# Later rounding and subtraction of the gated tokens, a shared ring of four activation buffers, and operands in a pool of their own

## The chip, the core and the metric

The kernel runs on one core of a Trainium2 chip. The metric is the device time of one execution in microseconds (us). An execution is a little longer than the span of the trace, which runs from the core's first instruction to its last.

The core's engines work side by side, each through its own queue and in order: TensorE (PE in the profile; its weight loads are shown apart as PEld), VectorE (DVE), ScalarE (ACT), GpSimd (POOL) and SyncE (SP), which here issues most of the DMAs. An instruction at the head of a queue that waits for another engine holds up all that stands behind it on its own engine.

## What is computed

A long convolution by Fourier transforms, gated with x, and then two two-layer networks over 24,960 tokens of 128 features, with 2,048 hidden features each:

```python
y = irfft(rfft(x * v, n=2*S) * rfft(h_filt, n=2*S))[:, :S]   # (2, 12480, 128)
a = x * y                                                    # the gate
h = a @ w_in1                                                # 128 -> 2048
g = h * clip(h + 3, 0, 6) / 6
b = g @ w_out1                                               # 2048 -> 128
h = maximum(b @ w_in2, 0)
out = (h * h) @ w_out2
```

## The kernel before

**Up to about 465 us** the kernel computes the filter and the forward and middle transforms. What follows is one long loop, and the change lies in it.

**Tokens.** The last step of the convolution makes the tokens in 64 blocks j of 390. For a block, `combine` adds and subtracts two loaded halves (`pp`, `pn`; DVE for j below 3, POOL after), `s4` runs 8 small float32 matmuls into a PSUM bank `py` (the trace shows each as two, 16 in all), and `gate` (L530) multiplies `py` by x in place (DVE, L532) and rounds it to the tile's high part `oh` (ACT, L534). `gate_rest` (L536) subtracts that from `py` to get the low part `ol` (DVE, L540). The networks take tiles of 512 tokens (the first one 390, the last one 506), so a block may fall into two tiles, and some tiles need two new blocks.

**Steps.** A step n is one tile and one of 8 slices of 256 hidden features (`NP` = 8 steps a tile). In the loop at L721 a step stands in this order: `l1(n)` (6 matmuls into the bank `ph`: weights low by high part, high by low, high by high, for two halves), `l2(n - 3)` (6 matmuls into the tile's bank `acc`), `finish` of a tile, the jobs in `early_do`, `relu(n)` (ACT), `act(n)` (DVE), `split(n - 1)` (ACT rounds `gh`; DVE or POOL subtracts `gl`, L643), the jobs in `late_do`, and one piece of `late`, which decodes the second network's weights until about 860 us. The engines take these in that order, each its own.

**Tiles.** The first 14 tiles are of network 1 alone; after that tiles of network 1 and network 2 alternate, and at the end there are 14 of network 2.

**The jobs of a block** are set by a table (L558 to L584): `s4` begins at a step n0 + q of the tile before (n0 is that tile's first step), at one of three rates, and is done 1, 2 or 4 steps later, at step `done`. `gate` stands in `early_do` of `done`, `gate_rest` in `early_do` of the step after, or of `done` itself at rate 1. Rate 1 is used behind the first 14 tiles for the first block of a tile that needs two; there are ten such tiles, at n0 = 128, 192, 240, 288, 336, 384, 448, 496, 544 and 592. Among the first 14 tiles four with two blocks stand at n0 = 24, 48, 72 and 96; their first block is begun at n0 and done at n0 + 1.

**A shared bank.** `py` and `acc` share two PSUM banks (`bank`, L506). A tile's first `l2` (at step n0 + 3) can't begin before the block that last used its bank has been read for the last time, which `gate_rest` does.

**Buffers.** `relu` writes `r` (2 buffers), `act` writes `g` (2), `split` writes `gh` and `gl` (3 each). All of them, `oh`, `ol` and the loaded blocks lie in one pool, `moe`.

Of the kernel before, what the change touches and what calls it, by code (L numbers as in the profile page):

```python
# [7 lines left out]
F32 = mybir.dt.float32  # L8
F32R = mybir.dt.float32r
U32 = mybir.dt.uint32  # L10
AF = mybir.ActivationFunctionType
ALU = mybir.AluOpType
# [19 lines left out]
TM = 512  # L32
# [11 lines left out]
def tile_hyena_moe(ctx: ExitStack, tc, xg, vg, xT, pos, w1d, w2d, fmat, fwin, twc,  # L44
                   tws, twcf, twsf, dcs, inv, vtab, w_in1, w_out1, w_in2, w_out2, out):
    nc = tc.nc
# [234 lines left out]
    with tc.tile_pool(name="mlp", bufs=2, side="right") as mp, \  # L281
# [40 lines left out]
        for c in range(16):  # L322
# [10 lines left out]
            for q in range(4):  # L333
                ov = hs[q][:N1].rearrange("p d (h a) -> p a h d", h=2)
                src = fps[:N1, :, :, 32 * q:32 * q + 32]
# [32 lines left out]
    def idle(ps, count):  # L368
        for _ in range(count):
            nc.tensor.matmul(ps[:, 0, :TOK], wh[0][:, 0, :128], wh[0][:, 0, :TOK])  # L370
# [4 lines left out]
    with tc.tile_pool(name="cv_ps", bufs=4, space=PSUM) as vps:  # L375
# [17 lines left out]
        for i in range(NI + 2):  # L393
# [19 lines left out]
            elif late_rows:  # L413
                blk, h, sv = late_rows.pop(0)
# [4 lines left out]
            for t, f in ((a + 6, load), (a + 3, product)):  # L419
                g, s = divmod(t, 3)  # L420
# [21 lines left out]
    early.close()  # L442


    mo = ctx.enter_context(tc.tile_pool(name="moe", bufs=2))
    mps = ctx.enter_context(tc.tile_pool(name="moe_ps", bufs=2, space=PSUM))
    zt, pm, xin = {0: (za, zb)}, {}, {}

    def inputs(t):
        if (0, t) not in xin:  # L450
            xin[(0, t)] = tuple(mo.tile([128, TM], F32R, name=f"o{p}{t}", tag=f"o{p}", bufs=3)
                                for p in "hl")
        return xin[(0, t)]

    inputs(0)
    ends = [TOK]
    while ends[-1] < NTOK:
        ends.append(min(ends[-1] + TM, NTOK))
# [14 lines left out]
    LAG = 3  # L473
# [30 lines left out]
    py = {}  # L504
# [19 lines left out]
    def ranges(j):  # L524
        for t in range(NTI):
            lo, hi = max(TOK * j, begins[t]), min(TOK * j + TOK, ends[t])
            if lo < hi:
                yield t, slice(lo - TOK * j, hi - TOK * j), slice(lo - begins[t], hi - begins[t])

    def gate(j):  # L530
        ps = py[j]
        nc.vector.tensor_tensor(ps[:, :TOK], ps[:, :TOK], xt.pop(j), ALU.mult)  # L532
        for t, src, dst in ranges(j):
            nc.scalar.activation(inputs(t)[0][:, dst], ps[:, src], AF.Copy)  # L534

    def gate_rest(j):  # L536
        ps = py.pop(j)
        for t, src, dst in ranges(j):
            h, l = xin[(0, t)]
            nc.vector.tensor_tensor(l[:, dst], ps[:, src], h[:, dst].bitcast(F32),  # L540
                                    ALU.subtract)

    begun, early_do, late_do = {}, {}, {}

    def plan(table, n, f, *args):
        table.setdefault(n, []).append((f, args))
# [7 lines left out]
    for t in range(1, NTI):  # L554
        js = list(range(last[t - 1] + 1, last[t] + 1))
        i = place_of[(0, t - 1)]
        n0, fast = NP * i, place_of[(0, t)] == i + 1
        if t == 1:  # L558
            jobs = [(js[0], 2, 2, i + 1), (js[1], 4, 2, i + 1)]
        else:  # L560
            jobs = [(js[-1], 4, 2 if fast else 0, i + 1)]
            if len(js) > 1:
                jobs.insert(0, (js[0], 0, 2 if fast else 1, i))
        assert len(js) == len(jobs)
        for j, q, rate, k in jobs:
            n = n0 + q
            plan(begun, n, s4, j, k)
            begun[n][-1] += (rate,)
            done = n + (4, 2, 1)[rate]
            gated[j] = done  # L570
            plan(early_do, done, gate, j)
            plan(early_do, done + (rate != 1), gate_rest, j)
            if j < 3:
                lead = (2, 1)
            elif j < 4:
                lead = (6, 5)
            else:
                lead = (7, 5)
            for back in lead:
                plan(late_do, n - back, combining, j)  # L580
            if j == 3:
                plan(late_do, 0, loads, j)
            elif j > 3:
                plan(late_do, gated[j - 3] + 1, loads, j)  # L584
# [12 lines left out]
    ph, rs, gs, gh, acc = ({} for _ in range(5))  # L597
# [15 lines left out]

    def relu(n):
        w = size[steps[n][1]]
        r = mo.tile([128, 2, TM], F32, name=f"r{n}", tag="r", bufs=2)
        if steps[n][0] == 0:
            nc.scalar.activation(r[:, :, :w], ph[n][:, :, :w], AF.Relu, bias=three)  # L618
        else:
            nc.scalar.activation(r[:, :, :w], ph[n][:, :, :w], AF.Relu)  # L620
        rs[n] = r

    def act(n):
        w = size[steps[n][1]]
        r, pv = rs.pop(n)[:, :, :w], ph.pop(n)[:, :, :w]
        gt = mo.tile([128, 2, TM], F32, name=f"g{n}", tag="g", bufs=2)
        g = gt[:, :, :w]
        if steps[n][0] == 0:
            nc.vector.scalar_tensor_tensor(g, r, 6.0, pv, ALU.min, ALU.mult)  # L629
        else:  # L630

            nc.vector.scalar_tensor_tensor(g, pv, 0.0, r, ALU.max, ALU.mult)  # L632
        gs[n] = g

    def split(n):
        g, w = gs.pop(n), size[steps[n][1]]
        h = mo.tile([128, 2, TM], F32R, name=f"gh{n}", tag="gh", bufs=LAG)[:, :, :w]
        l = mo.tile([128, 2, TM], F32R, name=f"gl{n}", tag="gl", bufs=LAG)[:, :, :w]
        nc.scalar.activation(h, g, AF.Copy)  # L639
        on_vector = (0, 3, 6) if n < NP * AHEAD else (0, 2, 4, 6)  # L640

        eng = nc.vector if n < NP or steps[n][2] in on_vector else nc.gpsimd
        eng.tensor_tensor(l, g, h.bitcast(F32), ALU.subtract)  # L643
        gh[n] = (h, l)
# [55 lines left out]
    decode(2, 1)  # L700
    decode(0, 3)
    gate(0)
    gate_rest(0)
    idle(mps.tile([128, 2, 512], F32, name="idle1", tag="ph", bufs=3), 6)
    decode(1, 3)
    decode(2, 6)
# [14 lines left out]
    for n in range(len(steps) + LAG + 1):  # L721
        if n < len(steps):
            l, j, q = steps[n]
            l1(n)
        m = n - LAG
        if 0 <= m < len(steps):
            l2(m)
        if 0 <= m - 1 < len(steps) and steps[m - 1][2] == NP - 1:
            finish(*steps[m - 1][:2])
        for f, args in early_do.pop(n, ()):  # L730
            f(*args)
        if n < len(steps):
            if q == 6 and n + 2 < len(steps) and steps[n + 2][0] == 1:
                part1(steps[n + 2][1])
            relu(n)
            act(n)
        if 0 <= n - 1 < len(steps):
            split(n - 1)
        for f, args in late_do.pop(n, ()):
            f(*args)  # L740
        for _ in range(2 if n < 14 else 1):
            next(rest, None)
# [94 lines left out]
```

## Time and profile before

| what | us |
|---|---|
| median of 3 runs | 2806.07 (2804.76 to 2806.34) |
| the profiled execution, its own time | 2803.87 |
| its span | 2801.7 |
| PE busy | 2742.1 (98%) |
| DVE busy | 1994.6 (71%) |
| ACT busy | 1931.6 (69%) |
| POOL busy | 1508.3 (54%) |

In a row of the trace the columns are the start, the duration, the engine, the line, the operation, what it writes and reads, and how many; in brackets stands the idle time of the engine before it, with who ended it. A matmul of 512 columns is shown with 0.39 us although the next one starts about 0.23 us later: they are pipelined, and the ends are modelled. Busy shares are means over stages with different limits, so windows and single waits say more than the totals.

### The profile page before, as it was taken

Reading aid. Unit: us, or ns where it says so; the run is one execution under the profiler, and the core shown is the slowest. Engines: PE = TensorE matmul, PEld = TensorE weight load, DVE = VectorE, ACT = ScalarE, POOL = GpSimd, SP = SyncE. Lnnn points to the kernel's source line nnn. Section 1 sums busy time; section 2 is a strip of 40 time slices with the busy share of each in tenths; the row PEclk is TensorE's granted clock in tenths of the full one; section 3 lists DMA queues with packets and bytes.
Section 4 is the critical chain, followed back from the end, with each engine's and each line's share of the span. In section 5 each row is a group of like instructions: output and inputs, shape, how many; then the busy total and the mean of one; then the engine's idle time right before and its main releaser. Section 6 shows DMA issues by size and latency. Waiting matters only on the chain.

```text
span 2801.7 us, 34821 instructions
## 1 busy us (share of the span) xinstructions
PE 2742.1 (98%) x12862; PEld 2282.0 (81%) x12862; DVE 1994.6 (71%) x1976; ACT 1931.6 (69%) x2192; POOL 1508.3 (54%) x884
## 2 busy tenths in 40 slices
PE   7999998999999999999999999999999999999999
PEld 5899997777778888888888888888888888888887
DVE  6899998887876666666666666666666666666666
ACT  5445545666667777777777777777777777777776
POOL 3888884466565454444444444444545454444444
PEclk9999999999999999999999999999999999999999
DMA  3253535212111001010101010010101010000000
GB/s 120 85 165 109 149 112 123 79 31 71 40 32 34 25 18 35 18 35 18 35 18 35 19 35 19 25 29 25 29 25 29 25 29 4 8 8 12 12 12 16
DMA packets 136472, 122.35 MB, mean 44 GB/s; under 512 B 99370, under 2 KB 114798, under 8 KB 134894
## 3 DMA queue, kind: packets, MB, share of 16 engines
q1 hardware_dynamic: 127570, 86.27, 11.3%
q10 hardware_dynamic: 8732, 33.85, 4.4%
q8 instruction: 101, 1.65, 0.2%
q14 instruction: 69, 0.57, 0.1%
HBM read 83.68 MB, written 36.37 MB: 43 GB/s over the span
## 4 chain that ended last, share of the span: by engine, by line
PE 85%; DVE 6%; issue 3%; POOL 1%; ACT 1%; DMA 0%; POOLq 0%; DVEq 0%; ACTq 0%
PE acc L660 35%; PE ph L610 35%; PE p L225 7%; PE p L179 4%; PE py L517 3%; PE p L256 2%; DVE g L629 2%; DVE gl L643 1%; POOL gl L643 1%; ACT r L618 1%; ACT gh L639 0%; DVE wp L127 0%; DVE wa L114 0%; DVE py L532 0%; DVE a L198 0%
## 5 line engine op out<-in xcount | busy, mean ns | idle before, releaser
L643 POOL TENSOR_TENSOR gl<-g,gh 128x1024 fp32r<-128x1024 f32 (+2 forms) x401 | 970.7, 2421 | 1152.6 <-ACT gh L639 1101.0
L660 PE MATMUL acc<-gh,wp 128*128 128x512 f32 (+2 forms) x3136 | 878.7, 400 | 10.0 <-DVE ol L540 10.0
L639 ACT ACTIVATE gh<-g 128x1024 fp32r<-128x1024 f32 (+2 forms) x784 | 823.8, 1051 | 62.5 <-DVE g L629 36.2
L632 DVE SCALAR_TENSOR_TENSOR g<-ph,r 128x1024 f32<-128x1024 f32 (+2 forms) x392 | 477.9, 1219 | 363.6 <-POOL gl L643 268.1
L629 DVE SCALAR_TENSOR_TENSOR g<-r,ph 128x1024 f32<-128x1024 f32 (+2 forms) x392 | 475.9, 1214 | 361.9 <-POOL gl L643 276.5
L660 PEld LDWEIGHTS acc<-gh,wp 128*128 128x128 f32 x3136 | 577.9, 189 | 126.0 <-ACT gh L639 4.6
L618 ACT ACTIVATE r<-ph,three 128x1024 f32<-128x1024 f32 (+2 forms) x392 | 436.2, 1113 | 237.0 <-PE ph L610 232.4
L610 PE MATMUL ph<-oh,wp 128*128 128x512 f32 (+2 forms) x1568 | 573.3, 402 | 0.1
L610 PE MATMUL ph<-xh,wp 128*128 128x512 f32 (+2 forms) x1568 | 552.2, 393 | 0.0
L620 ACT ACTIVATE r<-ph 128x1024 f32<-128x1024 f32 (+2 forms) x392 | 401.8, 1025 | 177.2 <-PE ph L610 176.8
L660 PE MATMUL acc<-gl,wp 128*128 128x512 f32 (+2 forms) x1568 | 494.1, 396 | 8.6 <-POOL gl L643 8.1
L643 DVE TENSOR_TENSOR gl<-g,gh 128x1024 fp32r<-128x1024 f32 (+1 forms) x383 | 473.7, 1237 | 0.0
L660 PEld LDWEIGHTS acc<-gl,wp 128*128 128x128 f32 x1568 | 293.8, 189 | 83.3 <-POOL gl L643 14.8
L610 PEld LDWEIGHTS ph<-xh,wp 128*128 128x128 f32 x1568 | 294.4, 188 | 64.2
L610 PEld LDWEIGHTS ph<-oh,wp 128*128 128x128 f32 x1568 | 296.9, 189 | 59.6 <-ACT oh L534 0.4
L610 PE MATMUL ph<-ol,wp 128*128 128x512 f32 (+2 forms) x784 | 309.4, 395 | 4.0 <-DVE ol L540 4.0
L610 PE MATMUL ph<-xl,wp 128*128 128x512 f32 (+2 forms) x784 | 306.4, 391 | 0.0
L210 ACT ACTIVATE h<-a 128x720 fp32r<-128x720 f32 x96 | 77.3, 806 | 193.8 <-DVE a L198 163.5
L211 POOL TENSOR_TENSOR l<-a,h 128x720 fp32r<-128x720 f32 x96 | 167.7, 1747 | 63.7 <-ACT h L210 63.7
L610 PEld LDWEIGHTS ph<-ol,wp 128*128 128x128 f32 x784 | 148.5, 189 | 32.3 <-DVE ol L540 6.4
L610 PEld LDWEIGHTS ph<-xl,wp 128*128 128x128 f32 x784 | 147.4, 188 | 32.1
L534 ACT ACTIVATE oh<-py 128x390 fp32r<-128x390 f32 (+47 forms) x111 | 34.7, 357 | 152.0 <-DVE py L532 152.0
(97 smaller groups left out, 2699.2 us busy)
## 6 DMA issues: line engine op xcount, KB each, us to landing
zdb<-stg ACTq DMA_DIRECT2D x14, 1350.0 KB
x<-xg SPq DMA_DIRECT2D x64, 196.0 KB
v<-vg SPq DMA_DIRECT2D x64, 196.0 KB
xt<-xT SPq DMA_DIRECT2D x63, 195.0 KB
out<-ot ACTq DMA_DIRECT2D x47, 256.0 KB
za<-zdb SPq DMA_DIRECT2D x60, 180.0 KB
zb<-zdb SPq DMA_DIRECT2D x60, 180.0 KB
vt<-vtab SPq DMA_DIRECT2D x63, 137.8 KB
```

The lines of the kernel that those rows point to most:

```text
L179: nc.tensor.matmul(ps[:, c // 2, o:o + 2 * K1], src, fm if s else fw)
L211: nc.gpsimd.tensor_tensor(l, gt, h.bitcast(F32), ALU.subtract)
L225: nc.tensor.matmul(pv, wt, x, start=(n == 0), stop=(n == len(ops) - 1))
L517: nc.tensor.matmul(ps[:, o:o + n], pm[j][q][:, r, b, :], v[:, q, r, :n], start=(r == 0), stop=(r == 1))
L610: nc.tensor.matmul(ps[:, c, :w], wt, x[:, :w], start=(m == 0), stop=(m == 2))
L618: nc.scalar.activation(r[:, :, :w], ph[n][:, :, :w], AF.Relu, bias=three)
L620: nc.scalar.activation(r[:, :, :w], ph[n][:, :, :w], AF.Relu)
L629: nc.vector.scalar_tensor_tensor(g, r, 6.0, pv, ALU.min, ALU.mult)
L632: nc.vector.scalar_tensor_tensor(g, pv, 0.0, r, ALU.max, ALU.mult)
L639: nc.scalar.activation(h, g, AF.Copy)
L643: eng.tensor_tensor(l, g, h.bitcast(F32), ALU.subtract)
L660: nc.tensor.matmul(ps, wt, x, start=(q == 0 and m == 0), stop=(q == NP - 1 and m == len(ops) - 1))
```

## The change

`gate_rest` is split in two: `gate` keeps the multiplication alone, `gate_high` rounds (ACT), `gate_low` subtracts (DVE). `gate_high` goes to `late_do` of step `done`, behind that step's `relu`, `act` and `split`. `gate_low` goes to `early_do` of the step after, as before, but at rate 1 to `late_do` of `done`. Block 2's `s4` begins one step later (5 in place of 4). `act` writes over its input `r`, which gets 4 buffers; `g` is gone. `oh`, `ol`, `gh` and `gl` get the pool `operands`, opened ahead of `moe`.

```diff
+    op = ctx.enter_context(tc.tile_pool(name="operands", bufs=3))
     mo = ctx.enter_context(tc.tile_pool(name="moe", bufs=2))
...
     def gate(j):
         ps = py[j]
         nc.vector.tensor_tensor(ps[:, :TOK], ps[:, :TOK], xt.pop(j), ALU.mult)
+
+    def gate_high(j):
         for t, src, dst in ranges(j):
-            nc.scalar.activation(inputs(t)[0][:, dst], ps[:, src], AF.Copy)
-
-    def gate_rest(j):
+            nc.scalar.activation(inputs(t)[0][:, dst], py[j][:, src], AF.Copy)
+
+    def gate_low(j):
...
-            jobs = [(js[0], 2, 2, i + 1), (js[1], 4, 2, i + 1)]
+            jobs = [(js[0], 2, 2, i + 1), (js[1], 5, 2, i + 1)]
...
             plan(early_do, done, gate, j)
-            plan(early_do, done + (rate != 1), gate_rest, j)
+            plan(late_do, done, gate_high, j)
+            if rate == 1:
+                plan(late_do, done, gate_low, j)
+            else:
+                plan(early_do, done + 1, gate_low, j)
...
-        r = mo.tile([128, 2, TM], F32, name=f"r{n}", tag="r", bufs=2)
+        r = mo.tile([128, 2, TM], F32, name=f"r{n}", tag="r", bufs=4)
...
-        r, pv = rs.pop(n)[:, :, :w], ph.pop(n)[:, :, :w]
-        gt = mo.tile([128, 2, TM], F32, name=f"g{n}", tag="g", bufs=2)
-        g = gt[:, :, :w]
+        g, pv = rs.pop(n)[:, :, :w], ph.pop(n)[:, :, :w]
         if steps[n][0] == 0:
-            nc.vector.scalar_tensor_tensor(g, r, 6.0, pv, ALU.min, ALU.mult)
+            nc.vector.scalar_tensor_tensor(g, g, 6.0, pv, ALU.min, ALU.mult)
...
-        h = mo.tile([128, 2, TM], F32R, name=f"gh{n}", tag="gh", bufs=LAG)[:, :, :w]
-        l = mo.tile([128, 2, TM], F32R, name=f"gl{n}", tag="gl", bufs=LAG)[:, :, :w]
+        h = op.tile([128, 2, TM], F32R, name=f"gh{n}", tag="gh")[:, :, :w]
+        l = op.tile([128, 2, TM], F32R, name=f"gl{n}", tag="gl")[:, :, :w]
```

Where instructions come to stand shows best in the queues. A number behind `r`, `g`, `gh`, `gl` and `ph` is the step, one behind `py` the block, one behind `oh` and `ol` the tile. ScalarE at steps 24 to 26, where block 5 (first of a tile with two blocks, n0 = 24) is gated, before:

```order
L618 ACTIVATE r24_5074<-ph24_5052,three_67 128x1024
L639 ACTIVATE gh23_5078<-g23_5043 128x1024
L534 ACTIVATE oh4_4980<-py5_5056 128x390
L618 ACTIVATE r25_5098<-ph25_5083,three_67 128x1024
L639 ACTIVATE gh24_5102<-g24_5076 128x1024
L123 ACTIVATE wp2_4706<-wa2_1_4904 128x512
L618 ACTIVATE r26_5121<-ph26_5107,three_67 128x1024
```

The same place after:

```order
L624 ACTIVATE r24_5053<-ph24_5031,three_67 128x1024
L643 ACTIVATE gh23_5056<-r23_5021 128x1024
L624 ACTIVATE r25_5075<-ph25_5061,three_67 128x1024
L643 ACTIVATE gh24_5078<-r24_5053 128x1024
L536 ACTIVATE oh4_4969<-py5_5035 128x390
L123 ACTIVATE wp2_4697<-wa2_1_4888 128x512
L624 ACTIVATE r26_5098<-ph26_5084,three_67 128x1024
```

The rounding into `oh4` stood ahead of `r25` and `gh24` and now stands behind them. On VectorE the order at this place is as before.

VectorE at steps 192 to 195, where block 26 is gated at rate 1 (n0 = 192), before:

```order
L629 SCALAR_TENSOR_TENSOR g193_9413<-r193_9411,ph193_9394 128x1024
L643 TENSOR_TENSOR gl192_9416<-g192_9388,gh192_9415 128x1024
L532 TENSOR_TENSOR py26_9372<-py26_9372,xt26_8468 128x390
L540 TENSOR_TENSOR ol20_9186<-py26_9372,oh20_9185 128x390
L629 SCALAR_TENSOR_TENSOR g194_9437<-r194_9435,ph194_9419 128x1024
L629 SCALAR_TENSOR_TENSOR g195_9462<-r195_9460,ph195_9443 128x1024
```

The same place after:

```order
L633 SCALAR_TENSOR_TENSOR r193_9221<-r193_9221,ph193_9204 128x1024
L647 TENSOR_TENSOR gl192_9225<-r192_9197,gh192_9224 128x1024
L532 TENSOR_TENSOR py26_9183<-py26_9183,xt26_8317 128x390
L633 SCALAR_TENSOR_TENSOR r194_9242<-r194_9242,ph194_9228 128x1024
L542 TENSOR_TENSOR ol20_9012<-py26_9183,oh20_9011 128x390
L633 SCALAR_TENSOR_TENSOR r195_9268<-r195_9268,ph195_9251 128x1024
```

The subtraction into `ol20`, the last reader of `py26`, now stands behind the activation of step 194. On ScalarE the rounding into `oh20` moved there too, behind `r194` and `gh193`.

## Rows read from the trace of the kernel before

**Rows 1.** The page, part 1: span, and PE's busy time.

```profile
span 2801.7 us, 34821 instructions
PE 2742.1 (98%) x12862; PEld 2282.0 (81%) x12862; DVE 1994.6 (71%) x1976; ACT 1931.6 (69%) x2192; POOL 1508.3 (54%) x884
```

**Rows 2.** Windows: stretch, length, busy us by engine (instructions), granted clock, DMA share, GB/s.

```profile
core 0: us, PE busy (x) PEld busy (x) DVE busy (x) ACT busy (x) POOL busy (x), PEclk, DMA share, GB/s
500.00:860.00 360.00, 339.23 (x1570) 274.43 (x1569) 290.57 (x266) 247.73 (x284) 217.27 (x133) 0.99 0.18 47
550.00:600.00 50.00, 46.61 (x212) 37.30 (x211) 45.05 (x41) 34.30 (x40) 29.24 (x17) 0.97 0.17 41
860.00:2790.00 1930.00, 1929.68 (x8731) 1585.51 (x8731) 1276.34 (x1175) 1427.83 (x1548) 923.10 (x507) 1.00 0.08 22
490.70:497.00 6.30, 6.27 (x27) 6.30 (x28) 3.03 (x5) 1.65 (x2) 0.55 (x1) 0.57 0.85 186
530.60:534.00 3.40, 3.40 (x9) 2.73 (x10) 3.40 (x5) 2.10 (x3) 0.87 (x2) 0.56 0.00 0
```

**Rows 3.** Waits of PE in 500 to 860 us: total us, times, longest.

```profile
PE acc L660 <- DVE ol L540: 10.0, 4, 3.4
PE acc L660 <- POOL gl L643: 7.0, 11, 1.0
PE ph L610 <- DVE ol L540: 3.8, 1, 3.8
```

**Rows 4.** Waits of the other engines over the whole span.

```profile
DVE g L629 <- POOL gl L643: 276.5, 149, 2.6
ACT oh L534 <- DVE py L532: 152.0, 64, 4.5
```

**Rows 5.** Timeline at step 25: gate of block 5, and PE's wait behind it.

```profile
566.32 0.56 DVE L532 TENSOR_TENSOR py<-py,xt 128x390 f32<-128x390 f32 x1
...
566.91 0.50 ACT L534 ACTIVATE oh<-py 128x390 fp32r<-128x390 f32 x1 [3.82 <-DVE py L532]
...
567.31 1.11 ACT L618 ACTIVATE r<-ph,three 128x1024 f32<-128x1024 f32 x1
...
568.52 1.22 DVE L629 SCALAR_TENSOR_TENSOR g<-r,ph 128x1024 f32<-128x1024 f32 x1 [1.64 <-ACT r L618]
...
570.79 0.56 DVE L540 TENSOR_TENSOR ol<-py,oh 128x390 fp32r<-128x390 f32 x1
...
571.50 0.77 PE L660 MATMUL acc<-gh,wp 128*128 128x512 f32 x1 [2.76 <-DVE ol L540]
```

**Rows 6.** Timeline: a gate one tile later, POOL behind it, and PE's wait for POOL.

```profile
606.77 0.56 ACT L534 ACTIVATE oh<-py 128x220 fp32r<-128x220 f32 x2 [3.54 <-DVE py L532]
...
609.36 2.39 POOL L643 TENSOR_TENSOR gl<-g,gh 128x1024 fp32r<-128x1024 f32 x1 [6.10 <-ACT gh L639]
...
611.81 0.74 PE L660 MATMUL acc<-gl,wp 128*128 128x512 f32 x2 [0.69 <-POOL gl L643]
```

**Rows 7.** Line L114 (a piece of the weight decode), min/median/max ns, first and last start.

```profile
L114 DVE TENSOR_TENSOR wa<-wa,wg x8: 678/1764/2818, 523.5 to 789.3; 128x512 f32<-128x512 f32 x8
...
L114 DVE TENSOR_TENSOR room<-room x4: 684/692/693, 460.4 to 489.5; 128x512 f32<-128x512 f32 x4
```

**Rows 8.** Timeline at step 4: block 2's first matmul and what precedes it.

```profile
490.07 0.56 DVE L540 TENSOR_TENSOR ol<-py,oh 128x390 fp32r<-128x390 f32 x1
...
490.73 1.14 PE L517 MATMUL py<-vt,pp 90*128 90x98 f32 x4 [4.57 <-issue]
```

**Rows 9.** Timeline at steps 194 and 195: block 26 at rate 1, and the tile's first l2.

```profile
1089.91 0.40 PE L610 MATMUL ph<-oh,wp 128*128 128x512 f32 x1
...
1091.42 1.11 ACT L618 ACTIVATE r<-ph,three 128x1024 f32<-128x1024 f32 x1
...
1091.56 0.56 DVE L540 TENSOR_TENSOR ol<-py,oh 128x390 fp32r<-128x390 f32 x1 [0.56 <-ACT oh L534]
...
1092.42 1.06 ACT L639 ACTIVATE gh<-g 128x1024 fp32r<-128x1024 f32 x1
...
1092.92 1.09 PE L660 MATMUL acc<-gh,wp 128*128 128x512 f32 x4
```

More of the change, by code (lines that the diff above doesn't have):

```diff
@@ L450, in inputs @@
         if (0, t) not in xin:
-            xin[(0, t)] = tuple(mo.tile([128, TM], F32R, name=f"o{p}{t}", tag=f"o{p}", bufs=3)
+            xin[(0, t)] = tuple(op.tile([128, TM], F32R, name=f"o{p}{t}", tag=f"o{p}")
                                 for p in "hl")
         return xin[(0, t)]
-    inputs(0)
     ends = [TOK]
@@ L624, in act @@
         w = size[steps[n][1]]
-        r, pv = rs.pop(n)[:, :, :w], ph.pop(n)[:, :, :w]
-        gt = mo.tile([128, 2, TM], F32, name=f"g{n}", tag="g", bufs=2)
-        g = gt[:, :, :w]
+        g, pv = rs.pop(n)[:, :, :w], ph.pop(n)[:, :, :w]
         if steps[n][0] == 0:
-            nc.vector.scalar_tensor_tensor(g, r, 6.0, pv, ALU.min, ALU.mult)
+            nc.vector.scalar_tensor_tensor(g, g, 6.0, pv, ALU.min, ALU.mult)
         else:
-            nc.vector.scalar_tensor_tensor(g, pv, 0.0, r, ALU.max, ALU.mult)
+            nc.vector.scalar_tensor_tensor(g, pv, 0.0, g, ALU.max, ALU.mult)
         gs[n] = g
@@ L702, in tile_hyena_moe @@
     gate(0)
-    gate_rest(0)
+    gate_high(0)
+    gate_low(0)
     idle(mps.tile([128, 2, 512], F32, name="idle1", tag="ph", bufs=3), 6)
```

## The prediction

> **What bounds the kernel now.** I read the page's totals first, then windows, then PE's own waits, and last the timeline around a few of them. The totals say PE is busy 98% of the span [rows 1], which hides where it isn't. The windows show it: from 860 to 2790 us PE is busy 1929.68 of 1930 us at full clock, with a matmul every 1930/8731 = 0.221 us [rows 2]. In that stretch no other engine's delay matters as long as PE never waits. From 500 to 860 us PE is busy 339.23 of 360 us [rows 2]; the 20.8 us between have three names: 10.0 us in four waits of a tile's first `l2` for the subtraction `ol` (which frees the bank), 3.8 us in one wait of an `l1` for `ol` as its input, 7.0 us in eleven waits for POOL's `gl` [rows 3]. Before 500 us one wait stands out, 4.57 us ahead of block 2's `s4` [rows 8]. So the early stretch can be won, and the late one only lost.
>
> The big totals mislead. DVE waits 276.5 us for POOL's `gl` at L629, since `g` has two buffers [rows 4]; in the late stretch PE doesn't feel it, and the ring of four gets nothing for it there.
>
> **The cause of the early waits.** At step 25 ACT stood idle 3.82 us with `oh` at the head of its queue, until DVE had come to the gate; only then could `relu` run (567.31), DVE then waited 1.64 us for that `relu`, and the `ol` behind it came at 570.79, 2.76 us late for PE [rows 5]. Such heads of queue cost ACT 152.0 us in 64 waits [rows 4], one for each block. One tile later the same hold-up reached POOL: `oh` waited 3.54 us, POOL had nothing to subtract for 6.10 us, and PE waited 0.69 us for `gl` [rows 6].
>
> **The change, part by part.** No instruction is added or removed, so no engine gets more work.
>
> *A, the waits for `ol`.* With `oh` behind `relu` and `gh`, step 25's `relu` needs only its matmuls. The gate at 566.32 is then followed on DVE by `act` at once (566.9), `gl` (568.0) and `ol` at about 569.2, against 570.79, with 1.13 us for each of the two big ones, half of the way from 568.52 to 570.79 [rows 5]. PE restarted 0.71 us behind the start of `ol`, so about 569.9, which leaves 1.2 of 2.76 us. That is with DVE as late at the gate as before; its lateness came from the same kind of hold-up a tile earlier and from waits for POOL, which the ring ends, so I expect the gate itself 1 to 3 us sooner and this wait gone. Of the five waits, 13.8 us, I keep 2 us, most of it for the one at 530 us, where two decode pieces stand between `act` and `ol`. Three of the five are followed by a stretch in which the granted clock is mostly at the lower of its two levels (1.2 of 2.4 GHz), of which one is shown: granted clock 0.56, 9 matmuls in 3.40 us [rows 2], 9 x 0.221 = 2.0 at full clock, so 1.4 us each and 4.2 in all. Gain of A: 11.8 + 4.2 = 16.0; bounds 7 and 18.
>
> *B, the waits for `gl`.* 7.0 us [rows 3]; where `gh` comes 3 us sooner POOL is done before PE asks. The modelled end of a matmul (0.40 us [rows 9] against 0.221) also hides 0.18 us in each of the 16 waits of A and B, 2.9 us. I take 5 of the 7 and 1.5 of the 2.9: 6.5; bounds 2 and 9.9.
>
> *C, block 2 a step later.* At step 4 PE waited 4.57 us, until the `ol` of block 1 (490.07) had freed the bank [rows 8], and then ran 6.3 us at a granted clock of 0.57, again mostly the lower level [rows 2]. Now an `l1` and an `l2` of 390 columns (12 matmuls at an estimated 0.221 x 390/512 = 0.17 us) stand ahead of that wait, 2 us, and `ol` should come about 1.4 us sooner without the hold-up of `relu`. Against that, `ol` of block 2 now comes one step before tile 1 needs it, and PE may wait there about 1 us. I take a gain of 4, half of it the shorter half-clock stretch; bounds 0 and 8.
>
> *D, rate 1.* Here is a loss. `gate_low` at rate 1 is the last reader of `py`, and now stands behind `act` of its step. At step 194 the last matmul of `l1` starts at 1089.91 and is over by about 1090.4; then ACT runs `relu` (1.00 to the next, from 1091.42 to 1092.42), `gh` (1.0) and `oh` (0.50), to 1092.9 [rows 5, 9]; `ol` starts there, and PE 0.71 us later, at 1093.6. Before, `ol` started at 1091.56, and PE began the tile's first `l2` at 1092.92 without a wait [rows 9]. So 0.7 us is lost, in a stretch where PE makes up nothing, and ten tiles have such a block: 7.0 us. Bounds 0 (if ACT gets to `oh` 0.7 us sooner than this) and 12.
>
> *E, the ring and the pools.* A step's `relu` needs the buffer of four steps earlier, whose `gl` was read by an `l2` that stands ahead of this step's `l1` on PE; so the ring adds no wait. The second pool moves `gh` and `gl` to other addresses. No row shows a matmul's pace hang on its operand's place: the late stretch has 0.221 us with operands in three buffers each. I take 0; a hundredth of that pace either way over the 9408 matmuls of the two networks would be 21 us, which I don't see a mechanism for and leave to the tails.
>
> **Sum.** -16.0 - 6.5 - 4 + 7.0 + 0 = -19.5 us. The profiled execution took 2803.87 us, 2.2 below the median of the runs, so it becomes 2784.4, and the median 2786.5. Forecast: **2786 us**, 0.7% faster. With all good ends it would be 2806 - 18 - 9.9 - 8 = 2770; with all bad ones 2806 - 7 - 2 + 12 = 2809.
>
> **Rivals.**
>
> *DVE stays full (2797).* In 550 to 600 us DVE is busy 45.05 of 50 us [rows 2]. Part of that is waiting that looks like work: L114 took 0.69 us on `room` but a median of 1.76 and up to 2.82 on `wa`, while POOL runs [rows 7]. If PE lost none of its 3.4 us in those 50, the same DVE work would have to fit into 46.6 us, 97% full, and any order on DVE would still be late somewhere. Then half of A and B goes, 11 us, and the result is 2786 + 11 = 2797. For it speaks that the decode is unchanged; against it, that DVE is busy only 290.57 of 360 us over the whole early part [rows 2]. The Trainium skill has a rule for this, in "SBUF — State Buffer", section "Who interferes with whom": a VectorE instruction with two SBUF inputs and a GpSimd one that reads SBUF share a port, and the second "fully blocks" until the first is done. The trace agrees: 2.82 - 0.69 = 2.1 us of blocking is close to one `gl` on POOL, 2.39 us. By the rule the blocked pieces stay as long as POOL subtracts, which the change doesn't touch; that is this rival, and its price is the one above.
>
> *The bank is the new wait (2813).* If the early hold-ups only change their name, with DVE late at `ol` because `oh` now comes a whole `relu` and `gh` later, then A, B and C bring nothing and D's 7 us stand alone: 2806 + 7 = 2813, slower. It decides at a gain of the early part under 7 us. Against it speaks the order on DVE at step 25, where `act` and `gl` stand between gate and `ol`, so `oh` has 2.3 us to be ready.
>
> *Nothing moves (2806).* PE is 98% busy; if the waits of the early part are made elsewhere by DMA or by the transforms' tail, the change shifts idle time and D is met by the slack. PE's waits have DVE and POOL as their names, not DMA, so I give it little.
>
> *D costs nothing (2779).* If `oh` gets done sooner than reckoned, the late loss is gone: 2786 - 7 = 2779.
>
> **How the numbers follow.** The forecast gets 0.60 (2780 to 2793), the full DVE 0.18, D for nothing 0.10, nothing moves 0.06, the bank alone 0.06. The range takes in the forecast, D for nothing and most of the full DVE: 2772 to 2799. A measurement of this kernel can tell about 0.2%, 5.6 us, from no change, so faster means under 2800.5: the forecast, D for nothing and three quarters of the full DVE, 0.84. Within 0.2% lie the rest of the full DVE and nothing moves, 0.10; slower is the bank alone, 0.06.
>
> **What would show it.** Right: ACT's waits for the gate at `oh` fall from 152 us to well under 100, PE's waits for `ol` in the early part fall under 4 us, its waits for `gl` under 3, and in the late part ten new waits of `acc` for `ol` of about 0.5 to 0.7 us appear, at n0 + 3 of the ten tiles. The stretch from 500 to 860 us shortens by 15 to 25 us while the late part grows by 7. Wrong: if PE still waits over 8 us for `ol` early (DVE stayed full), if the late part grows by over 12 us, or if the pace in the late part isn't 0.221 us a matmul.

## The result, and the profile after

The changed kernel takes **2773.2 us** (median of 4 runs, 2772.58 to 2773.49), beside 2805.41 for the kernel before: ratio 0.9886, interval 0.9869 to 0.9903, 32.2 us faster. The forecast was 2786 with a range of 2772 to 2799. The sign came out, and so did the mechanism of parts A to D; part E did not. The size was 13 us short, and the time lies 1 us inside the low end of the range. The profiled execution took 2773.49 us.

The page of the kernel after, part 1, answers to [rows 1]: PE is busy 98% as before, and in both traces this says nothing of the 30 us between them.

```profile
span 2771.5 us, 33774 instructions
PE 2728.0 (98%) x12862; PEld 2281.0 (82%) x12862; DVE 1999.9 (72%) x1976; ACT 1932.0 (70%) x2192; POOL 1594.2 (58%) x884
```

The windows of the early part of the kernel after (columns as in [rows 2]):

```profile
500.00:860.00 360.00, 355.60 (x1707) 297.92 (x1707) 312.45 (x282) 270.11 (x308) 240.95 (x146) 1.00 0.18 47
550.00:600.00 50.00, 49.84 (x242) 41.41 (x242) 49.41 (x44) 38.58 (x45) 32.62 (x19) 1.00 0.18 44
```

In the same 360 us PE now starts 1707 matmuls instead of 1570. Look at DVE in the second line: it is busy 49.41 of 50 us, fuller than before (45.05), and PE hardly stands still for it. That was one of the rivals, and it is weighed below.

The waits of PE, in 500 to 860 us (three rows) and behind 860 us (two), answer to [rows 3]; the rows of DVE and ACT behind them are of the whole span and answer to [rows 4]:

```profile
PE ph L616 <- DVE ol L542: 2.5, 1, 2.5
PE acc L664 <- DVE ol L542: 1.6, 2, 1.4
PE acc L664 <- POOL gl L647: 0.3, 1, 0.3
...
PE acc L664 <- DVE ol L542: 5.9, 10, 0.8
PE acc L664 <- POOL gl L647: 0.8, 1, 0.8
```

```profile
DVE r L633 <- ACT r L624: 345.1, 284, 2.5
...
ACT oh L536 <- DVE py L532: 3.0, 6, 0.8
```

ACT stood 152.0 us with `oh` at the head of its queue; now it is 3.0 us. PE's early waits fell from 20.8 to 4.4 us, and the ten late ones are new. DVE's waits for POOL, 276.5 us at one line, are gone; it waits for ACT's `relu` instead (69.1 us at that line before, 345.1 now).

To see where the 32 us lie I took from both traces the start of the first `l1` of every step, and added up the steps of a stage. The steps, not the clock time, have to be compared: at 860 us the two kernels aren't at the same work. The last line runs from the start of step 128 to that of step 783 (before: 895.62 to 2789.05 us, after: 863.08 to 2759.49). (e2 and e4 are experiments, told below.)

| us | before | after | e2_gate | e4_rate1 |
|---|---|---|---|---|
| to step 0 | 470.7 | 471.5 | 470.6 | 469.7 |
| steps 0 to 15 | 55.7 | 50.3 | 49.7 | 50.2 |
| steps 16 to 111 | 326.5 | 299.5 | 300.9 | 299.4 |
| steps 112 to 127 | 42.7 | 41.8 | 42.1 | 41.8 |
| steps 128 to 782 | 1893.4 | 1896.4 | 1901.2 | 1887.9 |

The first line differs between kernels whose code up to there is the same (469.6 to 472.1 over all traces of this study), so a difference of 2 us there between two single profiles needs no cause in the change. The last line is the surprise. Ten new waits stand in that stage, 5.9 us as recorded, and yet it grew by 3.0 us only. Something gave back a part of what they cost. The timeline shows what: the time from step to step. First matmuls of two successive steps without interpolation, in the first network (`oh`), of the kernel before and then of the kernel after:

```profile
1512.84 0.39 PE L610 MATMUL ph<-oh,wp 128*128 128x512 f32 x1
...
1515.62 0.39 PE L610 MATMUL ph<-oh,wp 128*128 128x512 f32 x1
```

```profile
1522.89 0.39 PE L616 MATMUL ph<-oh,wp 128*128 128x512 f32 x1
...
1525.62 0.39 PE L616 MATMUL ph<-oh,wp 128*128 128x512 f32 x1
```

Twelve matmuls took 2.78 us before and 2.72 to 2.73 after, with no wait in either: 231.7 and 226.6 ns from start to start. In the kernel before the distances within a step are uneven, 226 to 236 ns in an order that repeats from step to step; after, all twelve are 226 or 227. In the second network (`xh`) the steps stayed where they were, 2.77 to 2.78 us:

```profile
2690.31 0.40 PE L616 MATMUL ph<-xh,wp 128*128 128x512 f32 x1
...
2693.09 0.40 PE L616 MATMUL ph<-xh,wp 128*128 128x512 f32 x1
```

### The profile page after: what moved, and what is told of

The parts are those of the page before. It is cut to its first block, busy times and chain, and to the rows that moved or that the text cites. A ratio compares the mean times of both kernels' runs of the same rounds, so it can differ in the third digit from the quotient of the medians.

```text
span 2771.5 us, 33774 instructions
## 1 busy us (share of the span) xinstructions
PE 2728.0 (98%) x12862; PEld 2281.0 (82%) x12862; DVE 1999.9 (72%) x1976; ACT 1932.0 (70%) x2192; POOL 1594.2 (58%) x884
## 4 chain that ended last, share of the span: by engine, by line
PE 89%; DVE 6%; ACT 1%; issue 1%; POOL 0%; DMA 0%; POOLq 0%; ACTq 0%; DVEq 0%
PE ph L616 36%; PE acc L664 36%; PE p L225 7%; PE p L179 4%; PE py L517 3%; PE p L256 3%; DVE r L633 1%; DVE gl L647 1%; ACT gh L643 0%; ACT r L624 0%; DVE ol L542 0%; DVE wm L117 0%; DVE wa L114 0%; DVE wa L125 0%; DVE wa L108 0%
## 5 line engine op out<-in xcount | busy, mean ns | idle before, releaser
L647 POOL TENSOR_TENSOR gl<-r,gh 128x1024 fp32r<-128x1024 f32 (+2 forms) x401 | 966.9, 2411 | 1036.5 <-ACT gh L643 990.4
L643 ACT ACTIVATE gh<-r 128x1024 fp32r<-128x1024 f32 (+2 forms) x784 | 820.0, 1046 | 21.1 <-DVE r L633 20.5
L633 DVE SCALAR_TENSOR_TENSOR r<-r,ph 128x1024 f32<-128x1024 f32 (+2 forms) x392 | 475.3, 1213 | 345.6 <-ACT r L624 345.1
L636 DVE SCALAR_TENSOR_TENSOR r<-ph,r 128x1024 f32<-128x1024 f32 (+2 forms) x392 | 477.9, 1219 | 341.9 <-ACT r L626 341.7
L664 PE MATMUL acc<-gl,wp 128*128 128x512 f32 (+2 forms) x1568 | 484.5, 390 | 1.1 <-POOL gl L647 1.1
L647 DVE TENSOR_TENSOR gl<-r,gh 128x1024 fp32r<-128x1024 f32 (+1 forms) x383 | 473.8, 1237 | 0.0
L500 POOL TENSOR_TENSOR pp<-za,zb 90x256 f32<-90x256 f32 x122 | 135.2, 1128 | 37.8 <-PE ph L616 37.8
```

The lines of the kernel that those rows point to most:

```text
L500: eng.tensor_tensor((p, n)[k][:, :, r], za[:, :, r], zb[:, :, 1 - r], (ALU.add, ALU.subtract)[k])
L633: nc.vector.scalar_tensor_tensor(g, g, 6.0, pv, ALU.min, ALU.mult)
L636: nc.vector.scalar_tensor_tensor(g, pv, 0.0, g, ALU.max, ALU.mult)
L664: nc.tensor.matmul(ps, wt, x, start=(q == 0 and m == 0), stop=(q == NP - 1 and m == len(ops) - 1))
```

## The experiments

All times are medians, each beside runs of the kernel before on the same chip. The theory to begin with: the later gate brings A to C, rate 1 costs D, the ring nothing, and the pace comes with the pools. The rival: it is the ring, or all of it together.

**One part alone: the pool.** e1_pool is the kernel before with the tiles `oh`, `ol`, `gh` and `gl` in the pool `operands`:

```
+    op = ctx.enter_context(tc.tile_pool(name="operands", bufs=3))
...
+        h = op.tile([128, 2, TM], F32R, name=f"gh{n}", tag="gh")[:, :, :w]
+        l = op.tile([128, 2, TM], F32R, name=f"gl{n}", tag="gl")[:, :, :w]
```

> The kernel before with one part of the change: oh, ol, gh and gl in a pool opened ahead of the other; gate, r and g as before. Theory (the place of the operands sets the matmuls' pace): steps of network 1 without the gate's matmuls fall from 2.78 to 2.72 us as in the changed kernel, the early waits of PE stay (about 20 us from 500 to 860), and the time falls by about 11 us, to about 2794. Rival (the pace comes from when the engines issue, so from the gate or the ring): steps stay at 2.78 us and the time at 2805.

Measured: 2800.14 us, ratio 0.998 (0.9971 to 0.999). Half of the gain that was expected. Steps 128 to 782 took 1887.9 us, 5.5 less than before, and steps without interpolation 2.72 us: the quicker pace belongs to the pool alone. Of PE's waits in 500 to 860 us the one for POOL grew (7.0 us before):

```profile
PE acc L661 <- DVE ol L541: 10.4, 4, 3.5
PE acc L661 <- POOL gl L644: 9.7, 13, 1.1
PE ph L611 <- DVE ol L541: 3.8, 1, 3.8
```

In the early stage PE isn't the bound, so quicker matmuls there bring little: steps 16 to 111 took 329.3 us, 2.9 more than before. That they took longer can't be put down to the pace: e8_b64, below, has the same pace and 325.9 there, and e3_ring the old one and 329.3.

**One part alone: the gate.** e2_gate is the kernel before with `gate` split in three, `oh` and `ol` moved, and block 2 at step 5; old pools, old buffers:

```
-            plan(early_do, done + (rate != 1), gate_rest, j)
+            plan(late_do, done, gate_high, j)
+            if rate == 1:
+                plan(late_do, done, gate_low, j)
+            else:
+                plan(early_do, done + 1, gate_low, j)
```

> The kernel before with the gate's three parts moved and block 2's matmuls one step later; r, g and the pools as before. Theory (the early waits are the gate's hold-up on ScalarE): PE's waits from 500 to 860 us fall from 20.8 to about 4 to 8 us, ten late waits of about 0.57 us for ol appear, steps stay at 2.78 us, and the time is about 2806 - 22 - 5 + 7 = 2786. Rival (the ring is needed, since VectorE stays late behind POOL without it): PE keeps over 10 us of early waits and the time is 2795 or more.

Measured: 2780.03 us, ratio 0.9912 (0.9897 to 0.9927), 6 us less than expected. Of the early waits 2.6 us are left, with the old rings and pool (waits of PE in 500 to 860 us):

```profile
PE ph L616 <- DVE ol L542: 2.3, 1, 2.3
PE acc L666 <- POOL gl L649: 0.3, 1, 0.3
```

while DVE goes on waiting for POOL, at two lines, more than before (whole span):

```profile
DVE g L638 <- POOL gl L649: 331.2, 194, 2.1
DVE g L635 <- POOL gl L649: 284.7, 151, 2.5
```

**One part alone: the ring.**

```
-        r = mo.tile([128, 2, TM], F32, name=f"r{n}", tag="r", bufs=2)
+        r = mo.tile([128, 2, TM], F32, name=f"r{n}", tag="r", bufs=4)
...
-        gt = mo.tile([128, 2, TM], F32, name=f"g{n}", tag="g", bufs=2)
```

> The kernel before with one part of the change: activations written over r in a ring of four, g gone. Theory (PE doesn't feel VectorE's waits for POOL where it is the bound, and the early hold-up is the gate's): time 2800 to 2806, the early waits for ol stay above 10 us. Rival (VectorE's lateness early comes from its waits for POOL): early waits of PE fall by half and the time is about 2794. Second rival for the matmuls' pace: if it comes from the ring, steps fall to 2.72 us and the time to about 2794 with the early waits unchanged.

Measured: 2806.28 us, ratio 1.0003 (0.9993 to 1.0012). DVE's waits for POOL are gone from its list (it waits for ACT's `relu` instead, 365.3 us at L627), and PE gets nothing for it. The early waits of PE only change their names and add up to 22.9 us (500 to 860 us); those for `ol` are 9.8, just under the 10 expected:

```profile
PE acc L658 <- POOL gl L641: 7.4, 10, 1.3
PE acc L658 <- DVE ol L540: 6.0, 2, 3.3
PE acc L658 <- ACT gh L637: 5.7, 3, 3.7
PE ph L610 <- DVE ol L540: 3.8, 1, 3.8
```

So the two rows of 616 us of e2_gate and the time of e3_ring together say it: a wait of 276 us for POOL, on an engine that isn't the bound, is worth nothing that these runs can tell. No run puts the old rings back into the changed kernel. But e2_gate, which has neither ring nor pool, is 6.8 us slower than it, and the steps from 16 on hold 6.5 of them, most in the stage where the pace differs (4.8 from step 128 on), which leaves nothing of note to the ring.

**One part undone: rate 1.** e4_rate1 is the changed kernel with both halves of the gate of a rate-1 block back where they were:

```
-            plan(late_do, done, gate_high, j)
             if rate == 1:
-                plan(late_do, done, gate_low, j)
+                plan(early_do, done, gate_high, j)
+                plan(early_do, done, gate_low, j)
             else:
+                plan(late_do, done, gate_high, j)
                 plan(early_do, done + 1, gate_low, j)
```

> The changed kernel with the ten blocks of rate 1 rounded and subtracted where they were before (right behind the multiplication). Theory: the ten late waits of PE for ol (5.9 us of idle time, 0.73 us of a step each) go, nothing else moves, and the time is 2773 - 7 = 2766. Rival (PE makes the 0.7 us up elsewhere, or the hold-up of relu comes back in its place): 2771 to 2774.

Measured: 2763.28 us, ratio 0.9852 (0.9836 to 0.9869), 9.9 us less than the changed kernel. The stage from step 128 on got shorter by 8.5 of them (table); the rest is within what the start differs. The window of the kernel after and of e4_rate1 from 860 to 2700 us (length, then busy us of PE, PEld, DVE, ACT, POOL with counts):

```profile
860.00:2700.00 1840.00, 1834.06 (x8309) 1507.05 (x8308) 1214.38 (x1117) 1356.61 (x1470) 958.79 (x486) 1.00 0.08 23
```

```profile
860.00:2700.00 1840.00, 1840.00 (x8344) 1514.45 (x8343) 1217.98 (x1121) 1362.92 (x1477) 962.49 (x485) 1.00 0.08 23
```

The 5.94 us in which PE stood are gone. This version is faster than both kernels.

**What of the pool sets the pace?** The four tiles moved nearer to one another, but also to other places against the weights. By the addresses that the pools give out (bytes in a partition), `wp`, `oh` and `ol` lie a whole number of 2 KiB apart in both kernels. `gh` and `gl` join them in the changed one (110752 on); before, at 157024 on, they lay 192 bytes past a multiple of 256 from `wp`. `xh` and `xl` lie 64 past one in both. Theory: it is the place within some bytes. Rivals: the common pool or the nearness, or whole 2 KiB. Three kernels shift tiles by 64 bytes and do nothing else. e6_x64, on e4_rate1, moves `xh` and `xl`:

```
-            ot = mr.tile([128, TM], F32, name=f"ot{j}", tag="ot", bufs=1)
+            ot = mr.tile([128, TM + 16], F32, name=f"ot{j}", tag="ot", bufs=1)
```

> e4_rate1 with one edit: the tile ot is 64 bytes longer in each partition, so that the pool of the second side lies 64 bytes lower, and xh and xl with it (219040 instead of 219104). Then xh and xl lie a whole number of 256 bytes from the weights wp (16544), as oh, ol, gh and gl do in the changed kernel; before they lay 64 bytes beside it. No instruction is added, and what ot holds is the same. Theory (matmuls follow one another at 226.6 ns where all that TensorE reads in turn lies alike within 256 bytes, and at about 231 ns where it doesn't): a step of the second network without interpolation falls from 2.77 to 2.72 us, a tile of eight steps from 22.27 to about 21.8; with 49 such tiles -20 to -23 us against e4_rate1's 2763.3, so 2741 to 2744. Rival 1 (only a distance of whole 2 KiB counts, which oh, ol, gh and gl have and xh and xl still don't): 2763, the steps stay at 2.77. Rival 2 (it is the common pool or the nearness of the four tiles, not the place within some bytes): 2763.

Measured: **2744.42 us**, ratio 0.9781 (0.9767 to 0.9796): 64 bytes of an output tile are worth 18.9 us against e4_rate1, and the steps from 128 on hold 19.2 of them (1868.6 us). The second network's steps fell to 2.72 us (the kernel after has 2.78 at the same place, above):

```profile
2669.73 0.39 PE L617 MATMUL ph<-xh,wp 128*128 128x512 f32 x1
...
2672.45 0.39 PE L617 MATMUL ph<-xh,wp 128*128 128x512 f32 x1
```

`xh` and `xl` are 1792 bytes past a multiple of 2 KiB there, so whole 2 KiB aren't needed. e7_g64, on e4_rate1, moves `gh` and `gl` away, and e8_b64 moves them into line in the old pool of the kernel before (there `mo` for `op`):

```
+        if n == 0:
+            op.tile([128, 16], F32, name="gap", tag="gap", bufs=1)
         h = op.tile([128, 2, TM], F32R, name=f"gh{n}", tag="gh")[:, :, :w]
```

> e4_rate1 with one edit: an unused tile of 64 bytes in each partition stands between ol and gh in the operands' pool, so gh and gl lie 64 bytes higher (110816 instead of 110752) and no longer alike with wp, oh and ol within 128 bytes. No instruction is added. Theory (place within 128 or 256 bytes sets the pace): steps of the first network without interpolation go back from 2.72 to 2.78 us, those of the second from 2.77 to as before (22.23 a tile); about +10 us against e4_rate1's 2763.3, so 2771 to 2775. Rival (the common pool or the nearness sets it): 2763, the steps stay at 2.72.

> The kernel before with one edit: an unused tile of 64 bytes in each partition stands ahead of gh in the MLPs' pool, so gh and gl lie 64 bytes higher (157088 instead of 157024), a whole number of 256 bytes from wp, oh and ol, and still in another pool and far from them. No instruction is added or moved. Theory (place within 256 bytes sets the pace): the late steps of the first network without interpolation fall from 2.78 to 2.72 us as in e1_pool, whose median was 2800.1; so 2795 to 2801. Rival 1 (whole 2 KiB count): 2805, steps of 2.78. Rival 2 (the common pool or nearness): 2805, steps of 2.78.

Measured: e8_b64 2797.14 us, ratio 0.9971 (0.9959 to 0.9982), its steps 128 to 782 in 1887.9 us, just as e1_pool: the whole effect of the new pool on the pace, in the old one, by 64 bytes. Two successive first-network steps of e8_b64:

```profile
1510.94 0.39 PE L610 MATMUL ph<-oh,wp 128*128 128x512 f32 x1
...
1513.66 0.39 PE L610 MATMUL ph<-oh,wp 128*128 128x512 f32 x1
```

e7_g64 took 2760.09 us, ratio 0.9839 (0.9824 to 0.9853), a miss for both sides: 3 us faster than e4_rate1, where 10 slower was expected. Its steps in the first network did go back to 2.77 us. But in the second, where `gh` and `xh` were now alike and only `wp` was 64 bytes off, they fell to 2.75, which the theory hadn't reckoned with:

```profile
2682.42 0.39 PE L617 MATMUL ph<-xh,wp 128*128 128x512 f32 x1
...
2685.16 0.39 PE L617 MATMUL ph<-xh,wp 128*128 128x512 f32 x1
```

So the distance of each from each counts. e9_x192 asks for the grain, with 192 bytes in place of 64 in `ot`:

```
+            ot = mr.tile([128, TM + 48], F32, name=f"ot{j}", tag="ot", bufs=1)
```

> e6_x64 with one edit: ot is 192 bytes longer than in e4_rate1 instead of 64, so xh and xl lie 128 bytes lower than in e6_x64 (218912): alike with wp, oh, ol, gh and gl within 128 bytes, and 128 beside them within 256. It asks for the grain. Theory 128 (alike within 128 bytes is enough): steps of the second network stay at 2.72 us and the time at 2744 (2742 to 2747). Theory 256 (it must be alike within 256 bytes; for it speaks that in the kernel before gh and xh were alike within 128 and 128 apart within 256, and its tiles of the second network took 22.23, while in e7_g64, where they were alike within 256, they took 22.07): the steps go back to 2.75 to 2.78, so +10 to +22, 2754 to 2766.

Measured: 2759.95 us, ratio 0.9842 (0.9828 to 0.9857); steps of the second network at 2.77 us. 128 bytes off is as slow as 64 off.

```profile
2682.81 0.40 PE L617 MATMUL ph<-xh,wp 128*128 128x512 f32 x1
...
2685.58 0.40 PE L617 MATMUL ph<-xh,wp 128*128 128x512 f32 x1
```

e10_all64 moves everything but `xh` and `xl`, on e4_rate1:

```
     cp = ctx.enter_context(tc.tile_pool(name="const", bufs=1))
+    cp.tile([128, 16], F32, name="gap", tag="gap")
```

> e4_rate1 with one edit: an unused tile of 64 bytes in each partition stands first in the first pool, so that wp, oh, ol, gh and gl (and the buffers between) all lie 64 bytes higher, while xh and xl stay where they were in e4_rate1. All six are then alike within 256 bytes, as in e6_x64, each of them 64 bytes higher within 128 than there. Theory (only the distance between what TensorE reads in turn counts): 2744 as e6_x64 (2741 to 2748), steps of both networks 2.72 us. Rival (the place itself counts: 32 within 128 is quick and 96 slow): the steps of both networks at 2.77 to 2.78, so 2773 or more.

Measured: 2743.96 us, ratio 0.9783 (0.9768 to 0.9797), steps of 2.72 us in both networks. So the distances count and not the place itself, as far as one shift by 64 bytes can tell. The last two take the weights alone out of line, by 64 and by 128 bytes, with an unused tile first in the pool `operands` (and, for 128, `ot` as in e9_x192):

```
     op = ctx.enter_context(tc.tile_pool(name="operands", bufs=3))
+    op.tile([128, 16], F32, name="gap", tag="gap", bufs=1)
```

> e4_rate1 with one edit: an unused tile of 64 bytes in each partition stands first in the operands' pool, so oh, ol, gh and gl lie 64 bytes higher (98528, 110816, ...); xh and xl stay (219104). All that TensorE moves is then alike within 256 bytes, and the weights wp alone lie 64 bytes beside it. Theory 1 (weights and moving operands count alike, as in e7_g64, whose tiles of the second network were in this state and took 22.07 against 21.88): steps of about 2.75 us in both networks, +0.2 us in each of some 98 tiles against e6_x64, so 2757 to 2766. Theory 2 (only what is moved counts): steps of 2.72, 2742 to 2747. Theory 3 (the weights count most): steps of 2.77 or more, 2770 to 2775.

> As e12_w64 with 128 bytes for 64: the unused tile is 128 bytes, and ot 192 bytes longer, so that xh and xl (218912), oh, ol, gh and gl are alike within 256 bytes and the weights lie 128 bytes beside them. Theory (the weights' distance counts within 256 bytes, as that of xh did in e9_x192): steps of 2.75 us or more in both networks, 2755 to 2775. Rival (the weights don't count at 128): 2742 to 2747.

Measured: e12_w64 2756.74 us, ratio 0.983 (0.9814 to 0.9846), steps of 2.75 us in both networks, as theory 1 has it; e13_w128 2783.53 us, ratio 0.9925 (0.991 to 0.994), 8.5 beyond the end of what was expected, with most steps at 2.78 to 2.80 us, the slowest of all:

```profile
2705.91 0.40 PE L618 MATMUL ph<-xh,wp 128*128 128x512 f32 x1
...
2708.70 0.39 PE L618 MATMUL ph<-xh,wp 128*128 128x512 f32 x1
```

**One part undone: block 2.** e11_c4 is e6_x64 with the interpolation of block 2 at step 4 again:

```
-            jobs = [(js[0], 2, 2, i + 1), (js[1], 5, 2, i + 1)]
+            jobs = [(js[0], 2, 2, i + 1), (js[1], 4, 2, i + 1)]
```

> e6_x64 with one edit: the interpolation of block 2 starts again at step 4 instead of 5, as in the kernel before; nothing else of the changed kernel is undone. Theory (term C: with it at step 4, TensorE asks for weights and for block 2's operands before they are there): +4 to +5.4 us against e6_x64's 2744.4, so 2748 to 2750, and the long step is the fourth again (11 us of step 4 or near it). Rival (the later gate rounding alone covers it): 2743 to 2746.

Measured: 2748.1 us, ratio 0.9799 (0.9782 to 0.9815), 3.7 us more than e6_x64 (2746.65 to 2748.78 against 2742.75 to 2746.35). By the two traces, steps 0 to 15 took 2.4 us more (52.9 against 50.5). Step 4 is the long one again, 9.28 us, and PE waits there as in [rows 8], but 3.62 us instead of 4.57. Behind that wait the granted clock is again in part at the lower of its levels, 0.76 in 490 to 497 us:

```profile
490.13 0.66 PE L517 MATMUL py<-vt,pp 90*128 90x98 f32 x4 [3.62 <-issue]
```

```profile
490.00:497.00 7.00, 6.87 (x36) 6.90 (x37) 3.48 (x6) 2.15 (x3) 0.55 (x1) 0.76 0.80 198
```

The expectation named weights and operands that aren't there yet. The trace points at the bank: PE starts 0.66 us behind the start of block 1's `ol` in this kernel (489.47), before (490.07) and after (489.01 to 489.67).

## Why the prediction was right, and where it was short

**The sum.** It was worked out from the profiled run, -19.5 us; the two traces lie 30.2 us apart and the medians 32.2. By the steps, 7 of the 10.7 us between sum and traces lie in E, 3.1 in A and B, and 1.4 in C; D took 0.8 more than reckoned. That the time is still in the range owes something to luck: the misses together took up 13 of the 14 us between forecast and lower end. Of the signs that the prediction named, these came: ACT's wait at `oh` (3.0 us), PE's early waits for `gl` (0.3) and the ten late ones (0.59 on average). PE's early waits for `ol` are 4.1 us, just over the 4 named. Steps 16 to 127 are 27.9 us shorter, more than the 15 to 25 named for that stretch, and the stage behind grew by 3.0 instead of 7, because of E.

**A and B, the waits for `ol` and `gl`: right, and somewhat larger.** Predicted 16.0 + 6.5 = 22.5 us. In e2_gate, where the pace is the old one, steps 16 to 111 took 25.6 us less. The working at step 25 can be held against the trace; this is the counterpart of [rows 5] in the kernel after:

```profile
558.11 0.56 DVE L532 TENSOR_TENSOR py<-py,xt 128x390 f32<-128x390 f32 x1
...
558.58 1.21 DVE L633 SCALAR_TENSOR_TENSOR r<-r,ph 128x1024 f32<-128x1024 f32 x1
...
559.61 1.11 ACT L624 ACTIVATE r<-ph,three 128x1024 f32<-128x1024 f32 x1
559.71 1.21 DVE L647 TENSOR_TENSOR gl<-r,gh 128x1024 fp32r<-128x1024 f32 x1
...
560.85 0.55 DVE L542 TENSOR_TENSOR ol<-py,oh 128x390 fp32r<-128x390 f32 x1
...
561.54 1.17 PE L664 MATMUL acc<-gh,wp 128*128 128x512 f32 x4 [0.16 <-DVE ol L542]
```

Gate, `act`, `gl`, `ol`, PE, with `ol` 2.74 us behind the gate where 2.9 were reckoned. PE's wait is 0.16 us instead of 2.76. What the prediction kept, 2 us, most of it at the wait of step 16, is there: 2.5 us. Behind it one of the three stretches at the lower clock stays too, which the sum had counted as won: the granted clock is 0.76 there (window of the kernel after):

```profile
524.00:531.00 7.00, 6.36 (x21) 5.04 (x22) 7.00 (x9) 4.01 (x5) 2.93 (x3) 0.76 0.01 2
```

One reason in A was wrong: that DVE would be sooner because the ring ends its waits for POOL. e2_gate has the old two-buffer rings, 616 us of such waits, and nearly the same gain (25.6 us; the changed kernel has 27.0, of which E holds 1.5).

**C, block 2: right.** Predicted 4, bounds 0 and 8. Steps 0 to 15 took 5.4 us less; block 2's later start, undone alone, costs 3.7 by the medians and 2.4 by the steps (e11_c4). PE's wait for the bank fell from 4.57 to 1.16 us, and the stretch at the lower clock behind it, which the prediction had shorter, is gone (0.57 in [rows 2], 1.00 in the kernel after):

```profile
490.00:497.00 7.00, 7.00 (x45) 6.80 (x45) 6.97 (x12) 4.45 (x8) 0.28 (x1) 1.00 0.90 200
```

The wait of about 1 us foreseen at tile 1's `ol` is in the trace too, 1.01 us at 499.04.

**D, rate 1: right.** Predicted ten waits and 7.0 us, bounds 0 and 12. The trace has ten, 5.9 us as recorded. One of them, the counterpart of [rows 9]:

```profile
1058.21 1.12 ACT L624 ACTIVATE r<-ph,three 128x1024 f32<-128x1024 f32 x1 [1.40 <-PE ph L616]
...
1059.22 1.05 ACT L643 ACTIVATE gh<-r 128x1024 fp32r<-128x1024 f32 x1
...
1060.17 0.48 ACT L536 ACTIVATE oh<-py 128x390 fp32r<-128x390 f32 x1
...
1060.69 0.56 DVE L542 TENSOR_TENSOR ol<-py,oh 128x390 fp32r<-128x390 f32 x1
...
1061.40 1.15 PE L664 MATMUL acc<-gh,wp 128*128 128x512 f32 x4 [0.57 <-DVE ol L542]
```

`relu`, `gh`, `oh`, `ol` and the restart 0.71 us behind the start of `ol`, as in the working. By the starts of the steps the stage from step 128 on lost 7.8 us in e2_gate against before, and gave back 8.5 in e4_rate1 against after, 2.4 and 2.6 more than the waits recorded (5.4 and 5.9). The modelled end of a matmul (0.39 us, where the next starts after 0.227) hides about 0.16 in each wait, 1.6 of this; the prediction added that to the early ones, but not here.

**E, the pools: the step that failed.** The prediction took 0, with the reason that no row shows the pace hang on an operand's place, since it held with operands in three buffers each. But buffers of 2 or 4 KiB in a ring have the same place within 256 bytes, so that row couldn't have shown it. Measured: 5.5 us in the steps from 128 on (before against e4_rate1, and the same in e1_pool and e8_b64), and 1.5 more in steps 16 to 111 (e2_gate against e4_rate1, where the ring differs too), about 7 of the 10.7 us by which the sum was short. It is the net of two: from step 128 on, 23 tiles of the first network with the interpolation of one block fell from 23.97 to 23.71 us, and 47 of the second network rose from 22.20 to 22.25. The prediction named "if the pace in the late part isn't 0.221 us a matmul" as a sign against it; an average over a stage with interpolation in it was too coarse for that sign (1840/8309 is 0.221 in the kernel after, too), and the steps show it. "A hundredth of the pace" was priced at 21 us and left to the tails; 64 bytes in e6_x64 are worth 18.9. So that the late stretch could "only" be lost was wrong as well: PE was busy 1929.68 of 1930 us there, and still not at its quickest pace.

**The rivals.** *DVE stays full* foresaw that DVE would be 97% busy and late for it. It is 99% busy (49.41 of 50), and PE loses 0.16 us in these 50: being full didn't make DVE late there, where the order serves PE's needs first. By the Trainium skill, "SBUF — State Buffer", section "Who interferes with whom", a VectorE instruction with two SBUF inputs contends with a GpSimd one that reads SBUF, and the one that comes second is blocked until the first is done. The trace agrees: the piece at L125 took 2.25 us at 562.45, beside two `gl` on POOL (561.75, 5.21 us together), and 0.69 us at 494.73, with POOL idle. At one place the rival does hold, the wait of step 16. There a decode piece (L117), 0.42 us at 491.91, took 3.85 us while POOL was at work (before: 3.81, at 526.38), and `ol` stands behind it. That POOL holds it up is read from these durations; no run took the piece away:

```profile
520.41 3.85 DVE L117 TENSOR_SCALAR wm<-wa 128x512 uint32<-128x512 uint32 x1
...
524.19 0.62 DVE L542 TENSOR_TENSOR ol<-py,oh 128x244 fp32r<-128x244 f32 x2
...
524.64 0.50 PE L616 MATMUL ph<-ol,wp 128*128 128x512 f32 x1 [2.48 <-DVE ol L542]
```

That is 2.5 of the 4.4 us that are left early. *The bank is the new wait* and *nothing moves* are out by the 20.8 us of early waits that became 4.4. *D costs nothing* is out by the ten waits.

## What to carry to other kernels

An instruction that waits at the head of an in-order queue costs what is queued behind it; move it behind what is ready, then look for the places without slack where that makes it late (here rate 1: 9.9 us, had back by leaving those blocks alone). Compare the time from start to start of like matmuls whenever a change moves tiles: a fully busy engine can still run 2% below its pace (here 2.78 us a step where 2.72 is possible), and no wait shows it. If the distances within a step are uneven, try the operands' addresses, with a filler of 64 bytes.

## What the runs showed of the hardware

The pace of back-to-back matmuls (128x512, `fp32r`, weights loaded for each) hangs on where weights and moving operands lie against one another. Steps of twelve matmuls without interpolation or wait, at full granted clock; places are distances to the weights within 256 bytes, of what `l1` and what `l2` moves:

| l1, l2 | seen in | us a step |
|---|---|---|
| 0, 0 | after, e1, e4, e8, e9 (first network), e6, e10, e11 | 2.72 |
| 64, 64 | e7 (second network), e12 | 2.75 |
| 128, 128 | e13 | 2.78 to 2.80 |
| 0, 64 | e7 (first network) | 2.77 |
| 64, 0 | after, e1, e4, e8 (second network) | 2.77 |
| 128, 0 | e9 (second network) | 2.77 |
| 0, 192 | before, e2, e3 (first network) | 2.78 |
| 64, 192 | before, e2, e3 (second network) | 2.77 |

With the same order of work the kernel took from 2744.0 (e10_all64) to 2783.5 us (e13_w128), 1.4%, by addresses alone. That a multiple of 256 is enough and 128 isn't is shown (e6_x64, e9_x192), and that the place itself doesn't count for one shift of all by 64 bytes (e10_all64); multiples of 64 alone were tried. Why it is so isn't shown by any run here: no view tells what PE's reads wait for. The version e6_x64 (e10_all64 is level with it) is 61.9 us (2.2%) faster than the kernel before, and of this about 26 us are the addresses (7 in E and 18.9 in e6_x64).
